# A length-six DFT over the sequence chunks for the third and fourth batch of a retention and Fourier-mixing kernel

## The chip, the core and the metric

The kernel runs on one core of a Trainium2 chip. The metric is the device time of one execution in microseconds (us): 241.95 us is the median of three runs before the change (241.94 to 242.2). The engines are called as in the profile: PE is TensorE (matmuls), PEld its weight loads, DVE is VectorE, ACT is ScalarE, POOL is GpSimd, SP is SyncE, which issues most DMAs.

## The reference

Four batches, eight heads, 768 positions, head width 64. A retention recurrence gives y; its heads, side by side, are a matrix x of 768 rows and 512 columns per batch. Then comes a two-dimensional Fourier transform whose real part is added, a normalisation over the columns and a two-layer MLP of width 2048.

```python
for t in range(S):
    state = gamma[None, :, None, None] * state + np.einsum('bhd,bhe->bhde', k[:, :, t], v[:, :, t])
    y[:, :, t] = scale * np.einsum('bhd,bhde->bhe', q[:, :, t], state)
...
X = np.fft.fft(x, axis=1)
X = np.fft.fft(X, axis=2)
mixed = np.real(X).astype(np.float32)
u = x + mixed
mu = np.mean(u, axis=-1, keepdims=True)
var = np.mean((u - mu) ** 2, axis=-1, keepdims=True)
un = (u - mu) / np.sqrt(var + 1e-06)
ch = np.maximum(un @ w_ch1, 0.0) @ w_ch2
return (u + ch).astype(np.float32)
```

## The kernel before

The 768 rows are six chunks of 128 rows. Batch 0's attention comes first, in an order written out by hand. After that, period b (b = 0 to 3) runs the MLP of batch b on PE and, in between, attention and Fourier mixing of batch b + 1.

**The order.** `emit` collects units of work in streams, each with a first and last due time in periods, spreads a stream's units evenly over that time, and emits all units by due time. The MLP of one period is 58 units of major work: 16 `h_unit` (four matmuls into psh, L1087), one `rstd_unit`, 12 `ch_unit` (four matmuls into psc, L1130), and the same again for the second half of the rows. A 58th of a period is called a turn here. The steps of attention for batch b + 1 share one stretch of due times (`TS1`, from 0.048 to 0.633 of a period) in proportion to their number of units. A scheduler then gives each engine its instructions in order of emission among those that it takes to be ready; it decides this when the program is built, and an engine runs its list strictly in that order. In the trace, PE's order follows the due times: y of pair 2, due at turn 25.4, stands right after the major unit that is due at turn 25.

Attention works on four pairs of heads. `cast_unit` (POOL) makes f16 copies, `t_unit` transposes them (for batches 2 and 3 by DMA from SP's queue), `a_unit` makes the masked products atm (PE wkA L664, DVE L667), `kv_unit` the states s (PE wkK L683, ACT L689, DVE L693), `y_unit` the result (PE wkY L714 and L718), which ACT writes into x (L726).

**The fold.** With n = 128 c + p the position (chunk c, row p) and k the frequency, `fold_s` (DVE, L743) makes x[c] + x[c + 3] for even k and x[c] - x[c + 3] for odd k, three chunks of each: the tile ab, on two sides of the columns. It runs in two parts, one after the third pair of heads (step 4) and one after the fourth (step 5). `fold_d` (DVE, L770) adds and subtracts the two sides into eo, `fold_e` (DVE, L784 and L786) folds once more into ee, which takes over ab's memory. `g0_unit` treats the column 0 apart: small sums xg (L879, L882), nine small matmuls (L891) and the result g0 (L897, L900).

**First stage.** `s1_unit` multiplies ee by the cosine table csp or the sine table ssp (L847): per quarter (e, cb), for even and odd k, three chunks of 193 columns are summed in PSUM. ACT copies the 386 columns into g, even and odd k interleaved (L854), DVE writes the mirrored copy gr (L858).

**Second stage.** `s2_unit` transforms over the columns (PE pq L1009, ACT L1011 and L1012, DVE u L1016 and L1019, POOL u L1037 and L1039) for one block of 128 rows, `norm_unit` takes mean and variance (DVE bst L1049, L1050) and centres the row (ACT un L1051), `unT_unit` transposes it into unT (for batches 2 and 3 by DMA, L1070). The first three blocks of batch b + 1 come at the end of period b, since `h_unit` of period b + 1 needs all three of them; the other three follow in the period itself. On POOL the casts of the next attention stand behind the u sums, and on SP the transposition of their q (qTz, L609) stands in the same queue as unT.

**Evictions.** psh has three buffers. In the second half of the rows ACT (L1091) takes ten of the sixteen psh and DVE (L1093) rows 1, 2, 4, 5, 8 and 13. psc goes out through DVE (ob, L1134) and SP.

Of the kernel before, what the change touches and what calls it, by code (L numbers as in the profile page):

```python
# [11 lines left out]
AF = mybir.ActivationFunctionType  # L12
ALU = mybir.AluOpType
f32 = mybir.dt.float32
f16 = mybir.dt.float16
# [4 lines left out]
P = 128  # L20
# [5 lines left out]
NHP = H // 2  # L26
NK = 193
KN = 2 * NK
XW = 260
MAGIC = 12582912.0  # L30
PAIR_ORDER = [0, 1, 3, 2]
# [16 lines left out]
ON_ACT = {'q': (0, 1, 0), 'kv': (1, 1, 1), 'g': (0, 1, 1), 'gr': (0, 0, 0)}  # L48
# [5 lines left out]
LD0, LD1 = (0.223, 0.312), (-0.370, 0.140)  # L54
HT0 = (0.666, 0.693, 0.632, 0.590)
NPE = 2
KD = (2, 3)
NT = 0.6
ACT_ROWS = ((2, 5, 6, 7, 8, 9, 10, 14), (0, 3, 6, 7, 9, 10, 11, 12, 14, 15), (2, 4, 5, 6, 7, 8, 10, 11, 13, 14))
# [3 lines left out]
def kernel(  # L63
# [9 lines left out]
    nc = tc.nc  # L73
# [15 lines left out]
    gp = pool("gp", 1)  # L89
# [6 lines left out]
    ps_g = pool("ps_g", 5, space=PSUM)  # L96
# [7 lines left out]
    csp = const.tile([P, 2, 3, NK], f16, tag="csp")  # L104
    ssp = const.tile([P, 2, 3, NK], f16, tag="ssp")
# [58 lines left out]
    ht16 = hp_.tile([P, NFB, 384], f16, tag="ht16")  # L164
# [565 lines left out]
    fd = {}  # L730

    def fold_s(b, lo, hi, s0, s1):
        def run():
            x = xts[b % 2]
            if b not in fd:
                fd[b] = dict(
                    ab=fp.tile([P, 2, 3, 2, XW], f16, tag="xab", name="xab"),
                    eo=fp.tile([P, 2, 2, 3, 256], f16, tag="eo", name="eo"),
                    g=gp.tile([P, 4, KN], f16, tag="g16", name="g16"),
                    gr=gp.tile([P, 4, 384], f16, tag="g16r", name="g16r"))  # L740
            ab = fd[b]["ab"]
            for a, op in ((0, ALU.add), (1, ALU.subtract)):
                nc.vector.tensor_tensor(out=ab[:, a, :, s0:s1, lo:hi],  # L743
                                        in0=x[:, 0:3, s0:s1, lo:hi],
                                        in1=x[:, 3:6, s0:s1, lo:hi], op=op)
        return run

    def fold_p(i):
        def run():
            h = 2 * ORD0[i]  # L750
            if 0 not in fd:
                fd[0] = dict(
                    ab=fp.tile([P, 2, 3, 2, XW], f16, tag="xab", name="xab"),
                    g=gp.tile([P, 4, KN], f16, tag="g16", name="g16"),
                    gr=gp.tile([P, 4, 384], f16, tag="g16r", name="g16r"))
            x, ab = xts[0], fd[0]["ab"]
            side = h // 4
            lo, hi = {0: (1, 129), 2: (129, 258), 4: (130, 258), 6: (2, 130)}[h]
            for a, op in ((0, ALU.add), (1, ALU.subtract)):
                nc.vector.tensor_tensor(out=ab[:, a, :, side, lo:hi],  # L760
                                        in0=x[:, 0:3, side, lo:hi],
                                        in1=x[:, 3:6, side, lo:hi], op=op)
        return run

    def fold_d(b, cb, es=(0, 1)):
        def run():
            ab, eo = fd[b]["ab"], fd[b]["eo"]
            i0 = 2 + 128 * cb
            for e in es:
                nc.vector.tensor_tensor(out=eo[:, e, :, :, 128 * cb:128 * cb + 128],  # L770
                                        in0=ab[:, :, :, 0, i0:i0 + 128],
                                        in1=ab[:, :, :, 1, i0:i0 + 128],
                                        op=(ALU.add, ALU.subtract)[e])
        return run

    def fold_e(b, e):
# [56 lines left out]
    def s1e_unit(e, cb, eng):  # L833
        def run():
            gi = 2 * e + cb
            dst = fd[0]["g"][:, gi].rearrange("p (i t) -> p t i", t=2)
            (nc.scalar.copy if eng == "a" else nc.vector.tensor_copy)(dst, fd[0]["s1", e, cb])
        return run

    def s1_unit(b, e, cb):  # L840
        def run():
            eo, g, gr = fd[b]["eo"], fd[b]["g"], fd[b]["gr"]
            tab = csp if e == 0 else ssp
            ps = ps_g.tile([P, 2, NK], f32, tag="g", name="ps1", padded_shape=[P, 2, 256])
            for par in range(2):
                for sb in range(3):
                    nc.tensor.matmul(ps[:, par, :],  # L847
                                     fd[b]["ee"][:, 2 * e + cb, par, sb, :] if b >= FB else
                                     eo[:, e, par, sb, 128 * cb:128 * cb + 128],
                                     tab[:, par, sb, :], start=(sb == 0), stop=(sb == 2))  # L850
            gi = 2 * e + cb
            dst = g[:, gi].rearrange("p (i t) -> p t i", t=2)
            if e == 0 or ON_ACT["g"][min(b, 2)]:
                nc.scalar.copy(dst, ps)  # L854
            else:
                nc.vector.tensor_copy(dst, ps)
            if b:
                (nc.scalar.copy if ON_ACT["gr"][min(b, 2)] else nc.vector.tensor_copy)(  # L858
                    gr[:, gi], g[:, gi, 384:0:-1])
        return run  # L860
# [4 lines left out]
    def g0_unit(b, parts=(0, 1, 2)):  # L865
        def run():
            for part in parts:
                (g0_a, g0_b, g0_c)[part](b)
        return run
# [34 lines left out]
    lb = {}  # L904
# [177 lines left out]
    def h_unit(b, rt, fb):  # L1082
        def run():
            unT = lb[b]["unT"]
            psh = ps_pm.tile([P, 384], f32, tag="pm", name="psh", padded_shape=[P, DM])
            for cb in range(4):
                nc.tensor.matmul(psh, w116[:, cb, fb * P:(fb + 1) * P],  # L1087
                                 unT[:, cb, rt * 384:(rt + 1) * 384],
                                 start=(cb == 0), stop=(cb == 3))
            if fb in ACT_ROWS[2 if (b, rt) == (B - 1, 0) else rt]:  # L1090
                nc.scalar.activation(ht16[:, fb, :], psh, AF.Relu, bias=0.0, scale=-1.0)  # L1091
            else:
                nc.vector.tensor_scalar(out=ht16[:, fb, :], in0=psh, scalar1=-1.0, scalar2=0.0,  # L1093
                                        op0=ALU.mult, op1=ALU.max)
        return run
# [61 lines left out]
    def attn_steps(b):  # L1157
        steps = []
        for step in range(6):
            un = []  # L1160
            if step < 4:
                un.append(held(cast_unit(b, step)))
            i = step - 1
            if 0 <= i < 4:
                un.append(kv_unit(b, i))
            i = step - 2
            if 0 <= i < 4:
                un.append(y_unit(b, i))
                if i == 2:
                    un += [fold_s(b, 0, 130, 0, 2), fold_d(b, 0)]  # L1170
                    if b < FB:
                        un += [g0_unit(b), s1_unit(b, 0, 0), s1_unit(b, 1, 0)]
            if step < 4:
                un.append(t_unit(b, step))
            i = step - 1
            if 0 <= i < 4:
                if b == 0:
                    un += [a0_unit(b, i, 0), a0_unit(b, i, 1)]
                else:
                    un += [a_unit(b, i, part) for part in range(3)]  # L1180
            if step == 5:
                un += [fold_s(b, 130, 258, 0, 2), fold_d(b, 1)]
                if b >= FB:
                    un += [g0_unit(b), fold_e(b, 0), fold_e(b, 1)]
            steps.append(un)
        return steps

# [88 lines left out]
    for b in range(B):  # L1276
# [15 lines left out]
        if b + 1 < B:  # L1292
            steps = attn_steps(b + 1)
            if b == 0:
                streams.append(([load_unit(1, i, 6) for i in range(4)], LD0[0], LD0[1]))
                streams.append(([qt_zeros], 0.1, 0.15))
                streams.append(([half_tables], HT0[0], HT0[1]))
                streams.append(([pad_unit], HT0[2], HT0[3]))
                ts = TS0
            else:  # L1300
                streams.append(([load_unit(b + 1, i) for i in range(4)], b + LD1[0], b + LD1[1]))
                n = [len(u) for u in steps[1:]]
                ts = list(TS1[:2]) + [TS1[2] + TS1[3] * sum(n[:j]) / sum(n) for j in range(6)]
            streams.append((steps[0], b + ts[0], b + ts[1]))
            streams += [(u, b + ts[j + 2], b + ts[j + 3]) for j, u in enumerate(steps[1:])]
            end = b + ts[-1]
            da = DA0 if b == 0 else DA1
            streams.append(([s1_unit(b + 1, e, cb) for cb in range(2) for e in range(2)
                             if cb or b + 1 >= FB], end + da[0], end + da[1]))
            streams += mix_units(b + 1, [0, 1, 2], *(end + t for t in da[2:]))  # L1310
# [31 lines left out]
```

## Time and profile before

| what | value |
|---|---|
| median of three runs | 241.95 us |
| profiled execution, its own time | 242.19 us |
| span of the instructions in it | 240.2 us |
| granted TensorE clock | 1.00 |
| first-stage matmuls of batches 1, 2, 3 (L847) | 72 matmuls, 8.1 us in all |
| DVE fold of batches 1, 2, 3 (L743, L770, L784, L786) | 36 operations, 18.9 us in all |

The span counts from the first to the last instruction; the profiled execution's own time is that of the run in which the profile was taken. "x24" is a count, "mean ns" the duration of one; what stands in brackets behind an instruction is the idle time of its engine just before it and what ended that. Matmuls are pipelined, so a row's duration of one matmul is longer than its pace; the pace is read from the chain, which gives a run of matmuls as one piece.

### The profile page before, as it was taken

The numbers are of one execution on the slowest core, as the hardware profiler recorded it, in microseconds if no ns is written. First come the engines' busy times: TensorE is split into PE (matmuls) and PEld (weight loads), VectorE is DVE, ScalarE is ACT, GpSimd is POOL, SyncE is SP. The second block draws the span as 40 slices with busy tenths as digits, with TensorE's granted clock in tenths as the row PEclk, the third lists the DMA queues.
The fourth block names the chain that finished last, engine by engine and source line by source line (L and its number), as shares of the span: only waits on it lengthen the run. The fifth ranks groups of instructions, "written<-read, shape, count | busy, mean of one in ns | idle before, by whom it ended". The sixth has DMA issues, their size and how long they took to land.

```text
span 240.2 us, 5238 instructions
## 1 busy us (share of the span) xinstructions
PE 228.5 (95%) x1999; PEld 142.6 (59%) x1999; DVE 172.8 (72%) x419; ACT 120.8 (50%) x268; POOL 81.6 (34%) x148
## 2 busy tenths in 40 slices
PE   0888999999999999999999999999999999999994
PEld 0366779756774646665557446655675455446543
DVE  8789987968898789977995749977886557315121
ACT  5989759674865544941248406722366227203400
POOL 8377802675300097850001808930003224000000
PEclk9999999999999999999999999999999999999999
DMA  7999999999999399979999587675100331221012
GB/s 179 232 271 266 209 206 207 209 246 247 233 231 216 65 202 217 192 142 136 257 275 208 106 182 207 130 117 153 44 3 0 84 115 23 44 90 44 1 44 87
DMA packets 100808, 36.77 MB, mean 153 GB/s; under 512 B 91440, under 2 KB 97840, under 8 KB 100784
## 3 DMA queue, kind: packets, MB, share of 16 engines
q1 hardware_dynamic: 96560, 32.25, 63.7%
q0 software_dynamic: 4224, 4.19, 10.5%
q8 instruction: 15, 0.25, 0.4%
q14 instruction: 9, 0.07, 0.1%
HBM read 27.26 MB, written 6.29 MB: 140 GB/s over the span
## 4 chain that ended last, share of the span: by engine, by line
PE 83%; DVE 5%; SPq 5%; DMA 3%; POOL 2%; ACT 1%; issue 1%; ACTq 0%; POOLq 0%; DVEq 0%
PE psc L1130 34%; PE psh L1087 28%; SPq L216 5%; PE psh L1104 3%; PE wkA L664 3%; DMA q<-in_q_dram 3%; PE ps L847 3%; PE wkY L718 2%; PE pq L1009 2%; PE wkY L714 1%; PE wkK L683 1%; PE ps L827 1%; PE tq L620 1%; PE pst L1074 1%; DVE u L931 1%
## 5 line engine op out<-in xcount | busy, mean ns | idle before, releaser
L1130 PE MATMUL psc<-w,ht 128*128 128x512 f16 (+2 forms) x400 | 88.9, 370 | 0.0
L1087 PE MATMUL psh<-unT,w 128*128 128x384 f16 x448 | 81.6, 326 | 0.3 <-ACT ht L1091 0.3
L1130 PEld LDWEIGHTS <-ht 128*128 128x128 f16 x400 | 37.6, 98 | 36.8
L1087 PEld LDWEIGHTS <-w 128*128 128x128 f16 x448 | 42.1, 98 | 24.2 <-issue 0.8
L1091 ACT ACTIVATE ht<-psh 128x384 f16<-128x384 f32 x66 | 31.7, 490 | 41.2 <-PE psh L1087 40.3
L1037 POOL TENSOR_TENSOR u<-u,x 128x256 f32<-128x256 f32 x21 | 13.4, 636 | 107.1 <-DVE u L1016 95.0
L1134 DVE SCALAR_TENSOR_TENSOR ob<-psc,stats,u 128x512 f32<-128x512 f32 (+2 forms) x25 | 18.1, 724 | 29.0 <-PE psc L1130 28.9
L1093 DVE TENSOR_SCALAR ht<-psh 128x384 f16<-128x384 f32 x46 | 25.3, 549 | 8.9 <-PE psh L1087 8.5
L667 DVE TENSOR_TENSOR atm<-wkA,maskp 128x512 f16<-128x512 f32 x36 | 23.6, 681 | 1.5 <-PE wkA L664 1.5
L1051 ACT ACTIVATE un<-u,stats 128x512 f16<-128x512 f32 x21 | 14.8, 719 | 12.2 <-DVE stats L1050 8.2
L1049 DVE BATCH_NORM_STATS2 bst<-u 128x6 f32<-128x512 f32 x21 | 14.4, 687 | 4.9 <-POOL u L1039 4.7
L693 DVE SCALAR_TENSOR_TENSOR s<-s,gk,wkK 128x128 f16<-128x128 f16 x48 | 16.2, 337 | 2.4 <-ACT s L689 1.6
L726 ACT ACTIVATE x<-wkY,gexp 128x384 f16<-128x384 f32 x24 | 12.9, 581 | 9.0 <-PE wkY L718 8.9
L438 POOL TENSOR_SCALAR kd<-k,gexp 128x384 f16<-128x384 f32 x24 | 13.9, 589 | 3.4 <-DMA k<-in_k_dram 3.1
L1039 POOL TENSOR_TENSOR u<-u,x 128x256 f32<-128x256 f32 x21 | 13.3, 636 | 0.0
L664 PE MATMUL wkA<-qTz,kT 128*128 128x256 f16 x72 | 13.2, 272 | 0.1
L1011 ACT COPY qn<-pq 128x128 f32<-128x128 f32 x18 | 4.9, 274 | 13.7 <-PE pq L1009 13.6
L1104 PEld LDWEIGHTS <-w 128*128 128x128 f16 x192 | 11.0, 98 | 0.9 <-issue 0.5
L1104 PE MATMUL psh<-unT,w 128*128 128x128 f16 x192 | 11.4, 219 | 0.1
L1016 DVE SCALAR_TENSOR_TENSOR u<-pq,g,qn 128x256 f32<-128x256 f32 x18 | 8.5, 473 | 3.2 <-PE psh L1087 2.5
L443 POOL TENSOR_SCALAR v<-v 128x768 f16<-128x768 f32 x12 | 10.0, 834 | 1.5 <-DMA v<-in_v_dram 1.5
L664 PEld LDWEIGHTS <-kT 128*128 128x128 f16 x72 | 6.9, 98 | 5.6 <-issue 0.5
(175 smaller groups left out, 310.4 us busy)
## 6 DMA issues: line engine op xcount, KB each, us to landing
q<-in_q_dram SPq DMA_DIRECT2D x16, 384.0 KB, 6.0
k<-in_k_dram SPq DMA_DIRECT2D x16, 384.0 KB, 5.6
v<-in_v_dram SPq DMA_DIRECT2D x16, 384.0 KB, 6.2
out_dram<-ob SPq DMA_DIRECT2D x23, 256.0 KB, 2.4
w<-in_moe_w_ch_dram POOLq DMA_DIRECT2D x8, 512.0 KB, 10.7
unT<-un SPq DMA_TRANSPOSE x15, 2.4
out_dram<-ob SPq DMA_DIRECT2D x1, 192.0 KB, 1.9
kT<-kd SPq DMA_TRANSPOSE x10, 3.1
```

What stands on the lines that cost most here:

```text
L438: kc = nc.gpsimd.tensor_scalar(out=kd[:, :, h2, :], in0=k32[:, h2], scalar1=gkd[:, h0 + h2:h0 + h2 + 1], scalar2=1.0, op0=ALU.mult, op1=AL ...
L664: mm = nc.tensor.matmul(wk[:, c2], st["kT"][:, c, :], st["qT"][:, :, c, :], start=True, stop=True)
L667: nc.vector.tensor_tensor(out=st["atm"][:, 2 * part:2 * part + 2], in0=wk, in1=maskp[:, PAIR_ORDER[i]].unsqueeze(1).to_broadcast([P, 2, 2, ...
L693: nc.vector.scalar_tensor_tensor(out=s16[:, c], in0=s16[:, c - 1], scalar=gk2[:, hp:hp + 1], in1=wk[:, c - c0], op0=ALU.mult, op1=ALU.add)
L1049: nc.vector.bn_stats(bst, u[:, kb, :])
L1051: nc.scalar.activation(un, u[:, kb, :], AF.Identity, bias=stats[:, kb, 0:1], scale=-1.0)
L1087: nc.tensor.matmul(psh, w116[:, cb, fb * P:(fb + 1) * P], unT[:, cb, rt * 384:(rt + 1) * 384], start=(cb == 0), stop=(cb == 3))
L1091: nc.scalar.activation(ht16[:, fb, :], psh, AF.Relu, bias=0.0, scale=-1.0)
L1093: nc.vector.tensor_scalar(out=ht16[:, fb, :], in0=psh, scalar1=-1.0, scalar2=0.0, op0=ALU.mult, op1=ALU.max)
L1104: mm = nc.tensor.matmul(psh[:, f], w116[:, cb, fb * P:(fb + 1) * P], unT[:, cb, kb * P:(kb + 1) * P], start=(cb == 0), stop=(cb == 3))
L1130: nc.tensor.matmul(psc[:, c0:c1], ht16[:, fb, rb3 * P:(rb3 + 1) * P], w216[:, fb, c0:c1], start=(fb == 0), stop=(fb == NFB - 1))
L1134: nc.vector.scalar_tensor_tensor(out=ob[:, c0:c1], in0=psc[:, c0:c1], scalar=lb[b]["st"][:, rb, 3:4], in1=lb[b]["u"][:, rb, c0:c1], op0=AL ...
```

## The change

For batches 2 and 3 (`SIX = 2`) the sum over the chunks becomes a DFT of length six: with k = 6 j + r, the residue r alone decides how the six chunks are added, and one matmul per real or imaginary part with a table of 128 rows remains. `fold_s` stays and makes the first butterfly; the new `fold_six` makes the rest of it, in place in ab, one half of 128 columns at a time, between `fold_s` and `fold_d`. It has six DVE operations and one ACT copy per half. The first step of `g0_unit` (xg) moves ahead of the second `fold_six`, which overwrites what it reads. `s1_unit` multiplies by new tables: the first run of 65 columns belongs to r = 0 or 3, the other two runs of 130 to r = 2 and 4 or to r = 1 and 5. PSUM holds six runs of 65 columns, and ACT writes them into g at a step of six. The tables lie over the memory of csp and ssp for chunks 1 and 2, which nothing reads after batch 1; four units make them in period 1, due from 1.30 to 1.5, each with one POOL memset and four small ACT operations that stand behind the last ACT eviction of the first sixteen psh. All due times stay, but the three units that each of the two batches gains share the same stretch of `TS1`.

```diff
+KG = 390
+SIX = 2
+SIXP = 0
+ST0 = (1.30, 1.5)
...
-                    g=gp.tile([P, 4, KN], f16, tag="g16", name="g16"),
+                    g=gp.tile([P, 4, KG], f16, tag="g16", name="g16"),
...
+    def six_of(par):
+        return [t[:, par, 1:3].rearrange("p c k -> p (c k)") for t in (csp, ssp)]
+
+    def six_table(e, par):
+        def run():
...
+            to = six_of(par)[e]
...
+            nc.gpsimd.memset(to[:, 64:325], 0.0)
+            for out, in_, m in ((to[:, 0:65 - par], one, 1.0),
+                                (pairs[0], src[:, r0:r1 + 1:r1 - r0], 0.5),
+                                (pairs[1][:, 0], alt[:, r0], sg),
+                                (pairs[1][:, 1], alt[:, r1], -sg)):
+                if SIX > 1:
+                    with tc.issue_after(lb[SIX - 1]["relu"].ins):
+                        nc.scalar.activation(out, in_, AF.Copy, bias=0.0, scale=m)
...
+    def fold_six(b, half):
+        def run():
+            ab, eo = fd[b]["ab"], fd[b]["eo"]
+            c0 = 2 + 128 * half
+            a = [ab[:, :, c, :, c0:c0 + 128] for c in range(3)]
+            t = ab[:, :, 0, :, 2:130] if half else eo[:, 0, :, 0:2, 128:256]
+            nc.vector.tensor_tensor(out=t, in0=a[1], in1=a[2], op=ALU.add)
+            nc.vector.tensor_tensor(out=a[2], in0=a[1], in1=a[2], op=ALU.subtract)
+            for par, z, op, inv in ((0, t, ALU.subtract, ALU.add),
+                                    (1, a[2], ALU.add, ALU.subtract)):
+                (nc.gpsimd if SIXP else nc.vector).scalar_tensor_tensor(
+                    out=a[1][:, par], in0=a[0][:, par], scalar=2.0,
+                                               in1=z[:, par], op0=ALU.mult, op1=op)
+                nc.vector.tensor_tensor(out=a[0][:, par], in0=a[0][:, par], in1=z[:, par], op=inv)
+            nc.scalar.copy(a[2][:, 1], t[:, 1])
+        return run
...
+            if b >= SIX:
+                ps = ps_g.tile([P, 6, 65], f32, tag="g", name="ps1", padded_shape=[P, 6, 80])
+                for par in range(2):
+                    z, to = fd[b]["ee"][:, 2 * e + cb, par], six_of(par)[e]
+                    two = ps[:, 1:6:4] if par else ps[:, 2:5:2]
+                    for sb, (o, w, out) in enumerate(((0, 65, ps[:, 3 * par]), (65, 130, two),
+                                                      (195, 130, two))):
+                        nc.tensor.matmul(out, z[:, sb, :], to[:, o:o + w],
+                                         start=par == sb == 0, stop=par == 1 and sb == 2,
+                                         skip_group_check=True)
+                gi = 2 * e + cb
+                (nc.scalar.copy if e == 0 or ON_ACT["g"][min(b, 2)] else nc.vector.tensor_copy)(
+                    g[:, gi].rearrange("p (j r) -> p r j", r=6), ps)
...
-                    un += [fold_s(b, 0, 130, 0, 2), fold_d(b, 0)]
+                    un += [fold_s(b, 0, 130, 0, 2)]
+                    if b >= SIX:
+                        un.append(fold_six(b, 0))
+                    un.append(fold_d(b, 0))
...
-                un += [fold_s(b, 130, 258, 0, 2), fold_d(b, 1)]
+                un.append(fold_s(b, 130, 258, 0, 2))
+                if b >= SIX:
+                    un += [g0_unit(b, (0,)), fold_six(b, 1)]
+                un.append(fold_d(b, 1))
                 if b >= FB:
-                    un += [g0_unit(b), fold_e(b, 0), fold_e(b, 1)]
+                    un += [g0_unit(b, (1, 2) if b >= SIX else (0, 1, 2)), fold_e(b, 0),
+                           fold_e(b, 1)]
...
+                streams.append(([six_table(e, par) for e in range(2) for par in range(2)], *ST0))
```

More of the change, by code (lines that the diff above doesn't have):

```diff
@@ L753, in run @@
                     ab=fp.tile([P, 2, 3, 2, XW], f16, tag="xab", name="xab"),
-                    g=gp.tile([P, 4, KN], f16, tag="g16", name="g16"),
+                    g=gp.tile([P, 4, KG], f16, tag="g16", name="g16"),
                     gr=gp.tile([P, 4, 384], f16, tag="g16r", name="g16r"))
@@ L773, in run @@
                                         op=(ALU.add, ALU.subtract)[e])
+        return run
[3 more added lines that the diff above has]
+        def run():
+            same, other = (csp, ssp) if e == 0 else (ssp, csp)
+            sg = (-1.0 if e == 0 else 1.0) * math.sqrt(0.75)
+            to = six_of(par)[e]
+            src, alt = (t[:, par, 0, 0:192].rearrange("p (j r) -> p r j", r=3)
+                        for t in (same, other))
+            r0, r1 = ((1, 2), (0, 2))[par]
+            pairs = [to[:, o:o + 130].rearrange("p (r j) -> p r j", r=2)[:, :, 0:64]
+                     for o in (65, 195)]
+            one = same[:, 0, 0, 0:193:3] if par == 0 else src[:, 1]
+            nc.gpsimd.memset(to[:, 64:325], 0.0)
[6 more added lines that the diff above has]
+                        nc.scalar.activation(out, in_, AF.Copy, bias=0.0, scale=m)
+                else:
+                    nc.gpsimd.tensor_scalar(out=out, in0=in_, scalar1=m, scalar2=1.0,
+                                            op0=ALU.mult, op1=ALU.mult)
+        return run
@@ L835, in run @@
             gi = 2 * e + cb
-            dst = fd[0]["g"][:, gi].rearrange("p (i t) -> p t i", t=2)
+            dst = fd[0]["g"][:, gi, 0:KN].rearrange("p (i t) -> p t i", t=2)
             (nc.scalar.copy if eng == "a" else nc.vector.tensor_copy)(dst, fd[0]["s1", e, cb])
@@ L843, in run @@
             tab = csp if e == 0 else ssp
+            if b >= SIX:
[11 more added lines that the diff above has]
+                    g[:, gi].rearrange("p (j r) -> p r j", r=6), ps)
+                (nc.scalar.copy if ON_ACT["gr"][min(b, 2)] else nc.vector.tensor_copy)(
+                    gr[:, gi], g[:, gi, 384:0:-1])
+                return
             ps = ps_g.tile([P, 2, NK], f32, tag="g", name="ps1", padded_shape=[P, 2, 256])
@@ L851, in run @@
             gi = 2 * e + cb
-            dst = g[:, gi].rearrange("p (i t) -> p t i", t=2)
+            dst = g[:, gi, 0:KN].rearrange("p (i t) -> p t i", t=2)
             if e == 0 or ON_ACT["g"][min(b, 2)]:
@@ L1090, in run @@
             if fb in ACT_ROWS[2 if (b, rt) == (B - 1, 0) else rt]:
-                nc.scalar.activation(ht16[:, fb, :], psh, AF.Relu, bias=0.0, scale=-1.0)
+                relu = nc.scalar.activation(ht16[:, fb, :], psh, AF.Relu, bias=0.0, scale=-1.0)
+                if rt == 0:
+                    lb[b]["relu"] = relu
             else:
```

## The prediction

> **What bounds the kernel now.** I read the page's busy shares, the granted clock and the chain that ended last.
>
> ```profile
> span 240.2 us, 5238 instructions
> PE 228.5 (95%) x1999; PEld 142.6 (59%) x1999; DVE 172.8 (72%) x419; ACT 120.8 (50%) x268; POOL 81.6 (34%) x148
> PEclk9999999999999999999999999999999999999999
> PE 83%; DVE 5%; SPq 5%; DMA 3%; POOL 2%; ACT 1%; issue 1%; ACTq 0%; POOLq 0%; DVEq 0%
> ```
>
> TensorE bounds the span as a whole, at full clock. The change touches two stretches of it: the fold of batch 2, beside the major work of batch 1, and the fold of batch 3, beside that of batch 2. So next come the busy times by stretch (PE, PEld, DVE, ACT, POOL).
>
> ```profile
> 104.30:112.40 8.10, 8.10 (x68) 4.63 (x67) 5.29 (x12) 1.59 (x4) 1.00 (x2) 1.00 1.10 167
> 112.40:126.40 14.00, 13.94 (x127) 8.43 (x126) 12.84 (x31) 4.75 (x10) 0.00 (x0) 1.00 1.12 240
> 126.40:142.40 16.00, 16.00 (x102) 8.88 (x99) 8.38 (x22) 7.65 (x19) 6.54 (x11) 1.00 0.82 156
> 164.40:178.10 13.70, 13.70 (x127) 8.46 (x126) 12.69 (x31) 4.71 (x10) 0.00 (x0) 1.00 0.17 62
> ```
>
> While batch 2 is folded, PE has no gap, but VectorE is busy 12.84 of 14.00 us (batch 3: 12.69 of 13.70): nearly full too, and this is where the change adds VectorE work. Is anything of PE's waiting on the end of that fold? The first weight loads of the next batch's MLP answer it.
>
> ```profile
> 142.43 1.09 PEld L1087 LDWEIGHTS <-w 128*128 128x128 f16 x8 [0.39 <-DMA unT<-un]
> 193.89 1.29 PEld L1087 LDWEIGHTS <-w 128*128 128x128 f16 x8
> ```
>
> At 142.43 the loader of batch 2 stood 0.39 us for the transposed rows unT, with PE still fed by the matmul in the array. The chain behind unT, read back from there:
>
> ```profile
> 138.34 2.83 SPq L1070 DMA_TRANSPOSE unT<-un  x2
> 136.82 1.43 SPq L609 DMA_TRANSPOSE qTz<-q16z  x1
> 135.80 0.99 POOL L435 TENSOR_SCALAR q16z<-q 128x384 f16<-128x384 f32 x2
> 135.19 0.64 POOL L1039 TENSOR_TENSOR u<-u,x 128x256 f32<-128x256 f32 x1
> 133.41 0.64 POOL L1037 TENSOR_TENSOR u<-u,x 128x256 f32<-128x256 f32 x1 [1.19 <-DVE u L1016]
> 132.26 0.69 DVE L1049 BATCH_NORM_STATS2 bst<-u 128x6 f32<-128x512 f32 x1 [0.49 <-POOL u L1039]
> 130.43 0.48 DVE L1016 SCALAR_TENSOR_TENSOR u<-pq,g,qn 128x256 f32<-128x256 f32 x1 [1.27 <-PE psh L1087]
> 129.37 0.39 PE L1009 MATMUL pq<-gk,g 128*128 128x129 f16 x4
> 126.73 2.13 ACT L854 CAST g<-ps 128x386 f16<-128x386 f32 x4
> 125.87 0.56 DVE L786 TENSOR_TENSOR ee<-eo 128x768 f16<-128x768 f16 x1
> ```
>
> The last fold result ee is done at 126.43, the first second-stage product starts at 129.37, the u of the third block leaves POOL at 135.83, its casts hold the SP queue's qTz until 136.82, and both unT stand behind qTz. So for batch 2 the unT chain and PE arrive together: slack 0. For batch 3 the last unT is issued at 191.11:
>
> ```profile
> 191.11 1.22 SPq L1070 DMA_TRANSPOSE unT<-un  x1
> DMA to landing us min/median/max: 2.4/2.4/2.5
> ```
>
> It lands at 193.5, and the loader at 193.89 waited for nothing: slack about 0.35 us. My reading is that each period ends at the later of two things: PE's own work and the landing of unT.
>
> **The change part by part.** *First-stage matmuls.* 24 per batch stay 24; 193 columns become 65 (8 of them) or 130 (16).
>
> ```profile
> 126.18 2.05 PE ps L847 x24
> 113.31 0.35 PE wkY L718 x12
> 38.62 7.27 PE psh L1104 x128
> 112.15 0.86 PE psc L1130 x4
> L847 PEld LDWEIGHTS <-ee 128*128 128x128 f16 x72 | 6.1, 98 | 0.7 <-DVE ee L784 0.5
> L847 PE MATMUL ps<-csp,ee 128*128 128x193 f16 x36 | 4.1, 248 | 0.0
> ```
>
> Each of these loads weights of its own. 64 columns come at 0.35/12 = 29 ns, 128 at 7.27/128 = 57 ns. A quarter (six matmuls) is then 2 x 29.6 + 4 x 57.7 = 0.29 us, 1.16 per batch against 2.05: PE saves 0.89 a batch, 1.78 in all. [...]
>
> *VectorE.* Per half of 128 frequencies fold_six adds two adds of 512 elements, two of 256, two scalar_tensor_tensor of 256, and one ACT copy of 256 that the next fold_d waits for. Nothing is removed.
>
> ```profile
> L770 DVE TENSOR_TENSOR eo<-xab 128x768 f16<-128x768 f16 x12 | 6.1, 552 | 0.1
> L760 DVE TENSOR_TENSOR xab<-x 128x384 f16<-128x384 f16 x6 | 1.9, 357 | 0.3 <-ACT x L596 0.2
> 115.68 1.03 DVE L770 TENSOR_TENSOR eo<-xab 128x768 f16<-128x768 f16 x2
> L1016 DVE SCALAR_TENSOR_TENSOR u<-pq,g,qn 128x256 f32<-128x256 f32 x18 | 8.5, 473 | 3.2 <-PE psh L1087 2.5 <-ACT qn L1012 0.6
> L693 DVE SCALAR_TENSOR_TENSOR s<-s,gk,wkK 128x128 f16<-128x128 f16 x48 | 16.2, 337 | 2.4 <-ACT s L689 1.6
> L802 ACT ACTIVATE ht<-x 128x128 f16<-128x128 f16 x2 | 0.6, 304 | 0.0
> L508 ACT COPY kT<-tq 128x768 f16<-128x768 f16 x4 | 3.2, 802 | 0.0
> ```
>
> The adds cost (552 - 357)/384 = 0.51 ns an element: 422 ns at 512, 292 at 256. No all-f16 scalar_tensor_tensor is in the trace. Its bounds are 292 (as the add) and 473 (L1016); L693, partly f16, lies on the line of the f32 ones, so I take 473. Sum 2 x 422 + 2 x 292 + 2 x 473 = 2.37 us, less 0.074 of overlap each (two adds take 1.03, not 1.10) = 1.93 per half, 3.9 per batch. The copy is 304 + 128 x 0.78 = 0.40, with the two hand-overs about 0.5; in the first half atm products fill it, in the second nothing sure does. Total 4.4 us a batch.
>
> *What hides it.* The three extra units per batch squeeze the same stretch of due times: kv to fold of step 4 come due 1.5 to 1.9 turns earlier (y of pair 2 at 23.5 instead of 25.4 turns, fold_e unchanged at 36.7). At 0.86 us a turn the first half starts 1.6 us sooner, into VectorE time that is free (104.3 to 112.4: 5.29 of 8.10 busy). Another 0.7 is idle later:
>
> ```profile
> 120.69 0.56 DVE L1093 TENSOR_SCALAR ht<-psh 128x384 f16<-128x384 f32 x1 [0.69 <-PE psh L1087]
> ```
>
> So ee is late by 4.4 - 1.6 - 0.7 = 2.1 us. Between ee and pq lie 2.9 us now, with eight psh matmuls (1.3 us) in them. If those run before the late s1, pq follows ee after a quarter (0.29 + 0.25), a g copy (0.60) and a load: 1.2 us, and is late by 0.4; if PE's order stays, by 2.1 - 0.9 = 1.2. I take 0.8. From pq on the chain (POOL's six u sums, casts, qTz, unT) keeps its length, so unT is 0.8 late. Batch 2 has no slack: +0.8. Batch 3 has 0.35: +0.45. The saving of 1.78 is not collected, since PE would only stand longer for unT; it does pay for eviction waits of up to 1.7 us in the h phase, where fold_six stands before the L1093 evictions on VectorE and PE can run three psh ahead.
>
> *At nothing.* Sixteen table operations on ACT (up to 130 elements, so at most L802's 0.3 us, some 4 us together) and four memsets on POOL (261 elements, half of L243's 0.5 us) come due between turns 75 and 87, at least eight us ahead of use:
>
> ```profile
> 112.12 0.27 ACT L689 CAST s<-wkK 128x128 f16<-128x128 f32 x1 [4.30 <-issue]
> 118.46 0.49 ACT L1091 ACTIVATE ht<-psh 128x384 f16<-128x384 f32 x1 [3.88 <-PE psh L1087]
> L243 POOL MEMSET ht<- 128x512 f16 x1 | 0.5, 515 | 0.0
> 130.99 0.64 POOL L1037 TENSOR_TENSOR u<-u,x 128x256 f32<-128x256 f32 x1 [25.70 <-DVE u L1016]
> ```
>
> ACT idles 4.3 and 3.9 us there, POOL 25.7. Without that cover, all in front of one s copy, batch 2 would pay up to 4. The g copies take 390 elements for 386 with a wider output step: 0 to 0.1 us each, inside the 0.4 margin. The xg sums move ahead of fold_six: same count, no queue behind them but PE's nine small matmuls, now earlier.
>
> **Sum.** 242.19 (profiled execution, span 240.2) + 0.8 + 0.45 = 243.4; the median of the runs is 0.24 lower: 243.2.
>
> **The rivals.** *Faster, the saving arrives.* If the freed VectorE time takes both halves and the u sums close up (POOL stands 1.19 us before the second block at 133.41, because bst at 132.26 holds the next u behind it on VectorE), unT comes 0.9 earlier in both batches and PE collects 1.78: 240.2. It decides once pq is under 0.3 late and the gap closes. For it: that gap, and 2.8 free us before 112.4. Against: fold_six's second half has no earlier slot.
>
> *The scalar_tensor_tensor runs as fast as an add.* 292 instead of 473 ns, four a batch: 0.7 less, ee 1.4 late, unT 0.1: 242.19 + 0.1 - 0.25 - 0.24 = 241.8, no change. Against it L693's place on the slow line. [...]
>
> *VectorE becomes the bound.* If the earlier turns give nothing (wkA of pair 3 or y held by its own data), ee is 3.7 late, pq at least 2.0 in either order; +2.0 and +1.65: 245.6. It decides once ee comes over about 3 us late, since then all psh are done and PE has only psc and then unT. With no overlap of the operations and both copies exposed ee is 5.0 late: +3.3 and +2.95, 248.2. For it: 12.84 of 14.00 busy.
>
> *The matmuls don't get shorter.* If loads at 98 ns pace them, the last quarter is 0.3 longer: +0.3 a batch, 243.8. Against: 29 ns at 64 columns.
>
> **How the numbers follow.** Forecast 0.40 (own range 242.5 to 244.5), VectorE bound 0.20, saving arrives 0.24 (240.2 to 241.4), fast scalar_tensor_tensor or other cancelling 0.13, no shorter matmuls 0.03. 0.2% is 0.48 us, about what this kernel's runs can tell. Faster 0.26, the same 0.14, slower 0.60. The range 240.4 to 246.6 leaves out the far ends of both.
>
> **What would show it.** Right: matmuls L847's successors at 29 and 58 ns pace; fold_six 1.9 us a half; ee about 2 us later against PE's turns; at the first h weights of batches 2 and 3 a loader wait for unT of over 1 us, now with PE idle. Wrong: no such wait (the saving then shows as PE's shorter path), PE idle in the h phase before an L1093 eviction (then VectorE bounds there), or ACT's table operations in front of an s copy.

## The result and the profile after

| | before | changed kernel |
|---|---|---|
| median of six runs | 241.99 us (241.82 to 242.2) | 253.17 us (251.11 to 255.26) |
| ratio | 1 | 1.0452, 95% interval 1.042 to 1.0483 |
| profiled execution, its own time | 242.19 us | 253.34 us |
| its span | 240.2 us | 251.2 us |

The change costs 11.2 us where 1.2 were forecast. The page of the changed kernel shows a dent in PE's clock that was not there before, and less of the ending chain on PE:

```profile
span 251.2 us, 5286 instructions
PE 231.5 (92%) x1999; PEld 141.8 (56%) x1999; DVE 180.6 (72%) x443; ACT 131.3 (52%) x288; POOL 82.7 (33%) x152
PEclk9999999999999999999997999999997999999999
PE 68%; DVE 13%; ACT 7%; DMA 5%; POOL 3%; issue 2%; SPq 1%; ACTq 0%; POOLq 0%; DVEq 0%
```

The two slices at 7 lie at about 135 and 192 us, where the first stage of batches 2 and 3 hands over to the second. The windows there (PE, PEld, DVE, ACT, POOL, granted clock):

```profile
128.30:137.50 9.20, 5.92 (x44) 3.44 (x43) 4.52 (x13) 7.42 (x11) 1.86 (x4) 0.81 0.83 150
185.50:194.10 8.60, 5.30 (x44) 3.19 (x43) 4.40 (x13) 7.38 (x11) 1.44 (x3) 0.88 0.00 0
```

PE stands 3.28 and 3.30 us there and then runs under a reduced clock, while ACT, which was busy 7.65 of 16.00 us in the corresponding stretch before, is the engine at work. What ACT does, in its timeline (start, duration; in brackets the idle time before):

```profile
128.30 1.48 ACT L903 CAST g<-ps 128x390 f16<-128x390 f32 x1 [0.30 <-PE ps L899]
129.40 0.70 ACT L1155 ACTIVATE ht<-psh 128x384 f16<-128x384 f32 x1
130.00 4.05 ACT L903 CAST g<-ps 128x390 f16<-128x390 f32 x3
134.43 0.27 ACT L1075 COPY qn<-pq 128x128 f32<-128x128 f32 x1 [0.38 <-PE pq L1073]
```

and who waits for it, on PE:

```profile
129.84 0.23 PE L1073 MATMUL pq<-gk,g 128*128 128x129 f16 x1
129.91 0.49 PE L1151 MATMUL psh<-unT,w 128*128 128x384 f16 x2
132.80 0.29 PE L1073 MATMUL pq<-gk,g 128*128 128x128 f16 x2 [2.40 <-ACT g L903]
132.93 0.32 PE L1151 MATMUL psh<-unT,w 128*128 128x384 f16 x1
134.10 0.29 PE L1073 MATMUL pq<-gk,g 128*128 128x128 f16 x1 [0.85 <-ACT g L903]
```

The groups by shape give the reason. The changed kernel's copy into g, beside the copy of the old form that batch 1 still makes (L918):

```profile
L903 ACT CAST g<-ps 128x390 f16<-128x390 f32 x8 | 11.1, 1581 | 0.6 <-PE ps L899 0.6
L918 ACT CAST g<-ps 128x386 f16<-128x386 f32 x4 | 2.2, 600 | 3.3 <-PE ps L911 3.3
```

390 elements at a step of six take 1.58 us, 386 at a step of two 0.60. All four quarters of a batch pass through this one engine, so by the durations the last g is some 4 x 0.98 = 3.9 us late. In the timeline, where the copies overlap and one eviction stands between them, the four take 5.75 us from 128.30 to 134.05, for 2.13 before: 3.6 us. The other pieces came as costed or a little below:

```profile
L813 DVE TENSOR_TENSOR xab<-xab 128x512 f16<-128x512 f16 x2 | 0.8, 419 | 0.0
L817 DVE SCALAR_TENSOR_TENSOR xab<-xab 128x256 f16<-128x256 f16 x6 | 2.3, 418 | 0.0
L820 DVE TENSOR_TENSOR xab<-xab 128x256 f16<-128x256 f16 x6 | 1.5, 284 | 0.0
L821 ACT COPY xab<-eo 128x256 f16<-128x256 f16 x2 | 0.8, 405 | 7.5 <-DVE xab L820 7.5
L801 ACT ACTIVATE ssp<-csp 128x64 f16<-128x64 f16 x4 | 0.9, 261 | 0.0
```

One thing is left: the clock. One-us windows show it:

```profile
131.00:132.00 1.00, 0.00 (x0) 0.00 (x0) 0.26 (x1) 1.00 (x2) 0.00 (x0) 1.00 1.35 221
135.00:136.00 1.00, 1.00 (x8) 0.69 (x6) 0.78 (x2) 0.55 (x3) 0.53 (x1) 0.50 0.07 16
138.00:139.00 1.00, 1.00 (x6) 0.48 (x5) 0.95 (x4) 0.31 (x2) 0.49 (x2) 1.00 0.00 0
```

PE stands from 130.4 on but for 0.45 us of matmuls, and from 134.0 the granted clock is 0.50 for 3.41 us; the same from 192.0, after the second batch's copies. The 3.41 us ahead of the two falls:

```profile
130.57:133.98 3.41, 0.45 (x3) 0.17 (x3) 0.99 (x3) 3.41 (x3) 0.00 (x0) 1.00 1.11 200
188.59:192.00 3.41, 1.10 (x9) 0.64 (x10) 1.25 (x4) 3.09 (x5) 0.00 (x0) 1.00 0.00 0
```

In such a stretch four psh matmuls take 1.28 us of the chain (at 135.78), for 0.65 at full clock (at 60.63): half speed, and for 3.41 us of it 1.7 us of PE lost. So in this execution each batch pays about 3.3 for standing and 1.7 for the clock, 10.0 us for both. Another 0.67 is one wait of PE, in its timeline at the start of batch 2's fold:

```profile
116.01 0.38 PE L668 MATMUL wkA<-qTz,kT 128*128 128x256 f16 x2 [0.67 <-DMA qTz<-q16z]
```

That is 10.7 us, and the span is 10.9 longer than in run 1 below, whose copies alone differ (251.2 against 240.3). Beside the kernel before, where the spans are 11.0 apart, the count does not close: the shorter matmuls should have saved 1.78, and what takes that back is not in it.

### The profile page after: what moved, and what is told of

Read it like the earlier page. It is cut to its first block, busy times and chain, and to the rows that moved or that the text cites. A ratio compares the mean times of both kernels' runs of the same rounds, so it can differ in the third digit from the quotient of the medians.

```text
span 251.2 us, 5286 instructions
## 1 busy us (share of the span) xinstructions
PE 231.5 (92%) x1999; PEld 141.8 (56%) x1999; DVE 180.6 (72%) x443; ACT 131.3 (52%) x288; POOL 82.7 (33%) x152
## 4 chain that ended last, share of the span: by engine, by line
PE 68%; DVE 13%; ACT 7%; DMA 5%; POOL 3%; issue 2%; SPq 1%; ACTq 0%; POOLq 0%; DVEq 0%
PE psc L1196 28%; PE psh L1151 22%; ACT g L903 4%; PE psh L1170 3%; DMA v<-in_v_dram 3%; PE wkA L668 3%; DMA qTz<-q16z 3%; PE pq L1073 2%; PE wkY L722 2%; DVE xab L747 1%; DVE atm L671 1%; PE wkY L718 1%; SPq L220 1%; PE wkK L687 1%; PE ps L875 1%
## 5 line engine op out<-in xcount | busy, mean ns | idle before, releaser
L1196 PE MATMUL psc<-w,ht 128*128 128x512 f16 (+2 forms) x400 | 89.8, 373 | 0.0
L1151 PE MATMUL psh<-unT,w 128*128 128x384 f16 x448 | 84.4, 331 | 0.3 <-ACT ht L1155 0.3
L1159 DVE TENSOR_SCALAR ht<-psh 128x384 f16<-128x384 f32 x46 | 25.3, 550 | 8.4 <-PE psh L1151 8.0
L903 ACT CAST g<-ps 128x390 f16<-128x390 f32 x8 | 11.1, 1581 | 0.6 <-PE ps L899 0.6
L1073 PE MATMUL pq<-gk,g 128*128 128x128 f16 (+2 forms) x36 | 5.0, 261 | 6.6 <-ACT g L903 6.5
## 6 DMA issues: line engine op xcount, KB each, us to landing
w<-in_moe_w_ch_dram POOLq DMA_DIRECT2D x8, 512.0 KB, 10.7
out_dram<-ob SPq DMA_DIRECT2D x1, 192.0 KB, 1.9
```

Source lines behind the costliest of these rows:

```text
L903: (nc.scalar.copy if e == 0 or ON_ACT["g"][min(b, 2)] else nc.vector.tensor_copy)(g[:, gi].rearrange("p (j r) -> p r j", r=6), ps)
L1151: nc.tensor.matmul(psh, w116[:, cb, fb * P:(fb + 1) * P], unT[:, cb, rt * 384:(rt + 1) * 384], start=(cb == 0), stop=(cb == 3))
L1196: nc.tensor.matmul(psc[:, c0:c1], ht16[:, fb, rb3 * P:(rb3 + 1) * P], w216[:, fb, c0:c1], start=(fb == 0), stop=(fb == NFB - 1))
```

## The experiments

The theory after the result: the write of g at a step of six is dear, and almost all of the 11.2 us hangs on it. The rivals: fold_six on VectorE (the prediction's own mechanism), the tables, the clock by itself. Each run is compared with runs of the kernel before on the same chip, whose medians were about 242.2 us. Edits are against the changed kernel unless said otherwise.

**1. The copy turned round.** g is written at step one, and the step lies on the PSUM side.

```diff
-                    g[:, gi].rearrange("p (j r) -> p r j", r=6), ps)
+                    g[:, gi].rearrange("p (j r) -> p j r", r=6), ps.rearrange("p r j -> p j r"))
```

> The changed kernel, in which only the order of elements in ACT's copy of the first stage into g is turned round for batches 2 and 3: it writes g at a step of one element and reads PSUM at a step of one run, where it wrote at a step of six elements. Same elements, same 390, and the same order of instructions on all engines. Theory (the output step sets the copy's 1.58 us, and PE's wait for four such copies with the half clock that follows sets the loss): the copy falls to 0.7 us or less, no half clock in the fold stretches, time 241 to 244. Rival 1 (the late ee, from fold_six on VectorE, sets the loss and the copies only fill the same wait): the copy gets cheaper, but the time stays over 248. Rival 2 (PSUM's layout of six padded runs or their shortness sets the copy's price): the copy stays over 1.2 us and the time over 250.

Measured: 242.64 us (242.32 to 243.1), ratio 1.0017, 95% 1.0008 to 1.0026. The copy's group and the two windows in this kernel:

```profile
L903 ACT CAST g<-ps 128x390 f16<-128x390 f32 x8 | 3.5, 490 | 0.7 <-PE ps L899 0.6
128.30:137.50 9.20, 9.20 (x67) 5.00 (x67) 7.22 (x20) 5.94 (x16) 6.16 (x11) 1.00 0.78 146
185.50:194.10 8.60, 8.60 (x41) 3.92 (x40) 3.84 (x10) 2.25 (x4) 1.60 (x3) 1.00 0.40 108
```

The instructions and their order on every engine are those of the changed kernel; only the direction of eight copies differs. 1.58 us became 0.49, PE has no gap there, the clock stays at 1.00, and 253.17 - 242.64 = 10.5 us are gone. The copy's write is the cause, and the half clock came only with it.

**2. The dear write in the kernel before.** For batches 2 and 3 the old fold stays, but ACT writes 384 columns of g at a step of six, which puts them in another order.

```diff
-            dst = g[:, gi].rearrange("p (i t) -> p t i", t=2)
+            dst, ps = (g[:, gi].rearrange("p (i t) -> p t i", t=2), ps) if b < 2 else (g[:, gi, 0:384].rearrange("p (j t q) -> p t q j", t=2, q=3), ps[:, :, 0:192].rearrange("p t (q j) -> p t q j", q=3)); b < 2 or nc.gpsimd.memset(g[:, gi, 384:386], 0.0)
```

> The kernel before, in which for batches 2 and 3 ACT's copy into g writes 384 of the 386 columns at a step of six elements in six runs of 64 (the columns then stand in another order, so the result differs; POOL clears the last two). Nothing else of the change is in it. Theory: the copy takes 1.4 to 1.6 us instead of 0.60, pq comes some 3.5 us later, PE stands 2 to 3 us in each of the two batches and then runs at half clock for a few us; time 248 to 252. Rival 1 (fold_six sets the loss): under 244. Rival 2 (not the step, but the layout of the changed kernel's PSUM tile): copy under 0.8 us, time within 0.5 of before.

Measured: 248.56 us (247.18 to 251.08), ratio 1.0243, 95% 1.0213 to 1.0273. Groups and PE's waits in the profiled execution, which took 251.08 us:

```profile
L854 ACT CAST g<-ps 128x384 f16<-128x384 f32 x8 | 10.6, 1610 | 0.0
PE pq L1009 <- ACT g L854: 4.4, 4, 1.2
```

The step is dear without anything else of the change. Two of the four runs kept a mean granted clock of 1.000 and took 247.18 and 247.75 us, so without any half clock the cost is 5.0 to 5.5 us. The other two took 249.36 us at 0.993 and, in the profiled execution with two stretches of half clock of 3.41 us, 251.08 at 0.986. So the clock by itself, the last rival, is the smaller part.

**3. No fold_six, dear copy.** Both calls are left out, so the six chunks are not combined fully.

```diff
-                    if b >= SIX:
-                        un.append(fold_six(b, 0))
...
-                    un += [g0_unit(b, (0,)), fold_six(b, 1)]
+                    un += [g0_unit(b, (0,))]
```

> The changed kernel without fold_six (the other butterflies are left out, so the result differs); the new tables, shorter matmuls and the copy at a step of six stay. Theory (copies set the loss): copies still 1.5 us, ee some 2.5 us earlier, PE still waits for the copies, time 248 to 252. Rival 1 (fold_six sets the loss): 240 to 243.

Measured: 250.32 us (248.54 to 253.1), ratio 1.031, 95% 1.0283 to 1.0338; the copies still take 1.64 us each and PE still waits 6.0 us for them. Of the 11.2 us only some 2.9 go with fold_six, less than the spread of either kernel's runs, and most of the 2.9 is the clock: at the same mean clock of 0.993 the changed kernel took 251.11 us and this one 250.31 and 250.32, 0.8 apart. fold_six does not set the loss.

**4. No fold_six, copy turned round.** Edits 1 and 3 together.

> The changed kernel with the copy turned round as in the first of these runs and without fold_six (result differs): what is left are tables, shorter matmuls and the shifted due times. Theory: 240 to 241.5, the saving of PE as far as unT lets it through; the difference to the first run is the whole price of fold_six, 1 to 3 us. Rival (earlier due times or table operations cost something by themselves): over 242.

Measured: 241.83 us (241.5 to 243.55), ratio 0.9991, 95% 0.9978 to 1.0005. Beside run 1, fold_six costs 242.64 - 241.83 = 0.8 us for both batches. The tables, which are still made here, cost nothing that the time shows. Yet even without fold_six, little of the 1.78 us that PE saves arrives. The chain shows the saving, the loader's timeline one of the places where it ends:

```profile
126.25 1.20 PE ps L899 x24
141.63 1.09 PEld L1151 LDWEIGHTS <-w 128*128 128x128 f16 x8 [0.37 <-DMA unT<-un]
```

24 matmuls take 1.20 us, as costed (1.16). At the next batch's first weights PE is 0.80 us ahead of the kernel before, and its loader already waits for unT.

**5. fold_six's last copy on DVE.** With edit 1.

```diff
-            nc.scalar.copy(a[2][:, 1], t[:, 1])
+            nc.vector.tensor_copy(a[2][:, 1], t[:, 1])
```

> The first run's kernel (copy into g turned round), with the last copy of fold_six made by VectorE in place of ACT (4 copies of 256 f16 elements). Theory that the hand-over from VectorE to ACT and back delays the fold and keeps ACT from psh (ACT stood 7.5 us in all in front of these copies): ee 0.3 to 0.5 us earlier, 242.0 to 242.4. Rival (the hand-over is covered by atm and evictions, and VectorE only gets more to do): 242.5 to 242.9, as the first run.

Measured: 243.18 us (242.81 to 243.98), ratio 1.0037, 95% 1.0021 to 1.0053. The DVE copy takes 0.22 us for ACT's 0.41, and still nothing is gained, so the hand-over shows no cost of its own. The time is even 0.3 above the rival's range. A PE wait of 0.65 us for qTz, which run 1's profile does not have, is in this one; whether it makes the difference is not shown.

**6. Half of the dear copies on DVE.** Here the copies write at step six as in the changed kernel.

```diff
-                (nc.scalar.copy if e == 0 or ON_ACT["g"][min(b, 2)] else nc.vector.tensor_copy)(
+                (nc.scalar.copy if cb == 0 else nc.vector.tensor_copy)(
```

> The changed kernel as it is (copies still write g at a step of six), but two of the four copies of each batch, those with cb = 1, run on DVE. Theory A (the step-six write is dear on ACT alone, through its own write path): DVE's copies take 0.4 to 0.7 us, ACT's keep 1.6; the eight split 4 and 4, pq comes about 2 us earlier per batch than in the changed kernel, and the time is 245 to 247.5 us. Rival B (the price lies in the strided 16-bit write as such, whichever engine writes): DVE's copies take 1.2 us or more each, the two engines share the delay, and since DVE is nearly full there the time is 247 to 250 us. What decides is the duration of the DVE copies.

Measured: 248.05 us (247.61 to 248.79), ratio 1.0241, 95% 1.0222 to 1.026. The line's two groups (minimum, median and maximum in ns):

```profile
L903 ACT CAST g<-ps x4: 1454/1470/1487, 127.7 to 184.5; 128x390 f16<-128x390 f32 x4
L903 DVE CAST g<-ps x4: 1450/1451/1453, 129.4 to 186.3; 128x390 f16<-128x390 f32 x4
```

DVE pays 1.45 us for the same write, where its step-one evictions of 384 elements (L1159) take 0.55: the price is not ACT's alone. The mechanism and the time are B's. With two engines at the copies PE stands only 1.97 us in the ten from 128 on, and its clock stays at 1.00 there in the profiled execution:

```profile
128.00:138.00 10.00, 8.03 (x62) 4.30 (x61) 8.66 (x20) 5.82 (x12) 3.92 (x7) 1.00 0.63 118
```

**7. The due times as before.** Edit 1, and the three extra units of each batch are joined to their neighbours, so that nothing is squeezed.

```diff
-                        un.append(fold_six(b, 0))
+                        un.append(lambda u=un.pop(), w=fold_six(b, 0): (u(), w()))
...
-                    un += [g0_unit(b, (0,)), fold_six(b, 1)]
+                    un.append(lambda u=un.pop(), w=g0_unit(b, (0,)), z=fold_six(b, 1): (u(), w(), z()))
```

> The first run's kernel, with fold_six joined to fold_s (and to the first step of g0) in one unit, so that the attention steps of batches 2 and 3 keep the due times of the kernel before. Theory A (the squeezed due times cost PE 0.3 to 0.6 us a batch, because y now stands ahead of its last atm): PE's waits for atm go, 241.7 to 242.3. Theory B (the squeeze is what hides the first half of fold_six, as the prediction has it): ee comes over 1 us later than in the first run, unT with it, 243.3 to 245.

Measured: 245.03 us (244.79 to 245.96), ratio 1.0118, 95% 1.0093 to 1.0144. The loader, and the last ee of batch 2, first here and then in run 1:

```profile
144.03 1.09 PEld L1151 LDWEIGHTS <-w 128*128 128x128 f16 x8 [1.10 <-DMA unT<-un]
129.95 0.56 DVE L834 TENSOR_TENSOR ee<-eo 128x768 f16<-128x768 f16 x1
```

```profile
128.14 0.55 DVE L834 TENSOR_TENSOR ee<-eo 128x768 f16<-128x768 f16 x1
```

ee is 1.8 us later than with the squeeze, and the mechanism that the prediction described appears: unT is late and the next batch's weights wait 1.10 us for it. The earlier due times are worth 245.03 - 242.64 = 2.4 us.

**8. The kernel before with its copies turned round**, for batches 1 to 3.

```diff
-            dst = g[:, gi].rearrange("p (i t) -> p t i", t=2)
+            dst, ps = g[:, gi].rearrange("p (i t) -> p i t", t=2), ps.rearrange("p t i -> p i t")
```

> The kernel before, with ACT's copy of the first stage turned round in the same way for batches 1 to 3 (output at a step of one element in place of two). Theory (an output step of two already costs 0.1 us a copy, and the copies lie in front of unT, which has no slack for batch 2): copies 0.49 instead of 0.60, time 0.1 to 0.6 lower. Rival (PE's own work sets the end): copies cheaper, time the same within 0.1.

Measured: 242.13 us (241.78 to 242.78), ratio 0.9996, 95% 0.9983 to 1.001. The copies fall from 0.60 to 0.48 us, and nothing follows from it: a step of two was cheap enough to be hidden.

```profile
L854 ACT CAST g<-ps 128x386 f16<-128x386 f32 x12 | 5.8, 481 | 3.7 <-PE ps L847 3.4
```

**9. Steps of four and eight** in the kernel before, as in run 2 (`w` is 2 for batch 2, 4 for batch 3; one run).

```diff
-            dst = g[:, gi].rearrange("p (i t) -> p t i", t=2)
+            w = {2: 2, 3: 4}.get(b); dst, ps = (g[:, gi].rearrange("p (i t) -> p t i", t=2), ps) if b < 2 else (g[:, gi, 0:384].rearrange("p (j t q) -> p t q j", t=2, q=w), ps[:, :, 0:192].rearrange("p t (q j) -> p t q j", q=w)); b < 2 or nc.gpsimd.memset(g[:, gi, 384:386], 0.0)
```

> The kernel before, whose copy into g writes 384 columns at a step of four elements for batch 2 and of eight for batch 3 (the columns stand in another order, so the result differs). If the price grows with the step: 1.0 to 1.2 us at four, over 1.9 at eight. If there is a threshold between two and six: 0.6 at four and 1.6 at eight, or 1.6 at both. Time 245 to 256 by what the copies cost.

Measured: 249.66 us. The line's groups:

```profile
L854 ACT CAST g<-ps x4: 1019/1130/1138, 127.1 to 129.6; 128x384 f16<-128x384 f32 x4
L854 ACT CAST g<-ps x4: 1875/2198/2211, 179.9 to 184.7; 128x384 f16<-128x384 f32 x4
```

For 384 to 390 f16 elements the copy takes 0.49, 0.60, 1.13, 1.6 and 2.2 us at steps of 1, 2, 4, 6 and 8: beyond two it grows by about 0.27 us per element of step.

**10. The last batch alone.** Edit 1, and batch 2 keeps the old fold.

```diff
-SIX = 2
+SIX = 3
...
-ST0 = (1.30, 1.5)
+ST0 = (2.30, 2.5)
```

> The changed kernel with the g copies turned round (written at step one, PSUM read at step six) and the length-six DFT for the last batch alone; batch 2 keeps the old fold, and the tables are made in period 2 instead of period 1. Theory A (the periods' gains and losses add up as in the ledger of the run with both batches turned round: period 1 ends 0.4 us ahead, period 2 gives back 0.5): without the first batch's gain the time is 242.3 to 242.8 us, no better than before. Rival B (batch 3 has slack at its unT and could collect the shorter first stage once it doesn't start from a shifted schedule): 241.3 to 241.8 us, faster than both kernels. The eight copies become four of about 0.49 us at step one and four of 0.60 us at step two.

Measured: 242.87 us (242.43 to 243.77), ratio 1.0022, 95% 1.0011 to 1.0032. Rival B falls; batch 3's own slack does not let the saving through. A's figure holds but for 0.1 us.

**11. The shared due times begun earlier**, with edit 1.

```diff
-TS1 = (-0.040, -0.020, 0.048, 0.585)
+TS1 = (-0.040, -0.020, 0.025, 0.608)
```

> The changed kernel with the g copies turned round and the attention's shared stretch of due times begun 0.023 of a period (1.3 turns) earlier, with the same end, so that the three extra units of each batch no longer squeeze y against its atm. Theory A (of the 1.78 us that the shorter first stage saves, the squeeze costs about 0.9 and fold_six 0.8): the small waits of y for atm go, fold_six stays as early as with the squeeze, and the time is 241.4 to 242.1 us. Rival B (the earlier units wait for their own inputs, the casts of POOL and the transposed q and k of the DMA queue): PE waits there instead, 242.6 to 243.5 us.

Measured: 243.58 us (243.43 to 244.62), ratio 1.0057, 95% 1.0044 to 1.007. Worse, as rival B has it; PE's waits in the profile (us in all, times, longest; its execution took 244.62 us, the slowest of the six) name the inputs of both theories:

```profile
PE wkY L722 <- DVE atm L671: 0.7, 3, 0.3
PE wkA L668 <- DMA qTz<-q16z: 0.6, 1, 0.6
```

**12. Two evictions of the fold's stretch from DVE to ACT**, with edit 1.

```diff
-ACT_ROWS = ((2, 5, 6, 7, 8, 9, 10, 14), (0, 3, 6, 7, 9, 10, 11, 12, 14, 15), (2, 4, 5, 6, 7, 8, 10, 11, 13, 14))
+ACT_ROWS = ((2, 5, 6, 7, 8, 9, 10, 14), (0, 3, 4, 6, 7, 8, 9, 10, 11, 12, 14, 15), (2, 4, 5, 6, 7, 8, 10, 11, 13, 14))
```

> The changed kernel with the g copies turned round and rows 4 and 8 of the second sixteen psh evicted by ACT instead of DVE (0.50 us on ACT instead of 0.55 on DVE each), which takes 1.1 us off DVE between the two halves of fold_six. Theory A (VectorE's fullness in that stretch makes ee late and is what fold_six costs): ee comes 0.5 to 1.1 us earlier per batch, the psh behind them don't wait, and the time is 241.5 to 242.3 us. Rival B (ee was not what PE waited for once the copies are cheap, and ACT's evictions come later than DVE's did): no change or slower, 242.5 to 243.5 us.

Measured: 242.89 us (242.69 to 243.22), ratio 1.0028, 95% 1.0017 to 1.0039. The last ee of batch 2 comes 0.37 us before run 1's, not 0.5 to 1.1, and the time does not follow:

```profile
127.77 0.56 DVE L834 TENSOR_TENSOR ee<-eo 128x768 f16<-128x768 f16 x1
```

So no version that computes the whole reference beat the kernel before by a measurable amount.

## Why the prediction was wrong

The direction came true, the size did not: 253.17 against 243.2 and a range up to 246.6. By the prediction's steps:

- *"The g copies take 390 elements for 386 with a wider output step: 0 to 0.1 us each, inside the 0.4 margin."* **This step failed.** Each copy grew from 0.60 to 1.58 us, by 1.0, and its cover was gone at once, since the four copies of a batch follow one another on ACT with PE's pq behind the last. The runs put 10.5 us on it (run 1). The trace of before held a hint: the prediction's rows have L1091 at 0.49 us for 384 elements at step one, and the old copy at step two takes 0.60 (L918 above). Those 0.11 us per element of step, carried on to six, give 0.49 + 5 x 0.11 = 1.04: still too little, but far outside the margin. The bound of 0.1 had no row behind it.
- *The half clock* was no step of the prediction: after the start no row of before showed PE standing for long, and a stall was priced at its own length. In the profiled execution it came to half as much again.
- *Matmuls* at 29 and 58 ns: right, 24 in 1.20 us (run 4) for a predicted 1.16.
- *fold_six* at 1.93 us a half: right. The chain gives the first half of batch 3 in the changed kernel as 0.34 + 0.44 + 0.76 + 0.40 = 1.94:

```profile
172.15 0.34 DVE eo L813
172.52 0.44 DVE xab L814
172.98 0.76 DVE xab L817 x2
173.74 0.40 DVE xab L820 x2
```

  scalar_tensor_tensor lies at 418 ns, between the 292 and 473 taken as bounds and nearer to the one chosen; the rival in which it runs as fast as an add falls.
- *The squeeze hides the first half, and ee comes 2.1 us late*: right. With the copy mended ee ends at 128.69 against 126.43, 2.3 us late; without the squeeze (run 7) 4.1, where the time is 245.03. That is the rival "VectorE becomes the bound", which had 3.7 and 245.6 for this condition.
- *unT 0.8 and 0.45 us late, and PE waiting for it*: wrong but for run 7, where the weights waited 1.10 us. In the changed kernel PE itself was later than unT. In run 1, with the copy mended, the last unT of batch 2 were issued 0.85 us earlier than in the kernel before (137.49 for 138.34), and that of batch 3 0.45 earlier (190.66 for 191.11), although ee was 2.3 us late. That the chain from pq on "keeps its length" did not hold: POOL's 1.19 us of standing in front of the second block's u sums is gone, so the six run without a gap:

```profile
132.53 0.64 POOL L1101 TENSOR_TENSOR u<-u,x 128x256 f32<-128x256 f32 x1
137.49 2.85 SPq L1134 DMA_TRANSPOSE unT<-un  x2
```

  This is the condition of the rival "the saving arrives", and still PE did not collect.
- *The saving is not collected*: right in the outcome, but not for the reason given, since in run 1 nothing waits for unT. Even without fold_six only 0.2 to 0.4 us arrived, and that interval holds 1 (run 4).
- *Tables and memsets at nothing*: right, 0.25 to 0.33 us an operation on ACT. One copy of s (at 104.56) stands among them, which was named as a sign of being wrong, but no wait of PE for it is in the trace.

With the one step mended, the sum's 243.2 stands beside 242.64 measured in run 1. That is in part luck: the two terms that the sum adds, unT's 0.8 and 0.45, did not come. Where exactly run 1 spends the first stage's 1.78 us is settled only in part. Together with the 0.4 us by which run 1 is slower than the kernel before, some 2.2 us have to be found: 0.8 is fold_six, and 0.5 are waits of PE, which stands 0.55 us between 92 and 194 us, about half of it for atm in the squeezed stretch, where the kernel before stands 0.06. The rest stays open; the two attempts to win it back (runs 11 and 12) failed.

## What to carry to other kernels

A change of layout that only touches the address pattern of an eviction can have a price of its own (here 1.58 us a copy at step six for 0.60 at step two): find a row for that step, or bound it by the widest step the trace shows and carry the slope on; "a few elements more" is no bound. If a regrouping is needed, put the step on the PSUM side, where it cost nothing here (0.49 us a copy). And when several such copies stand in a row ahead of PE's next work, add to PE's stall the half clock that may follow it (here 1.7 us behind a stall of 3.3).

## What the runs showed of the hardware

- An f16 write into SBUF at a step cost both ACT and DVE time: 1.47 and 1.45 us for 390 elements at step six (run 6), and 0.49, 0.60, 1.13, 1.5 to 1.6 and 2.2 us on ACT at steps 1, 2, 4, 6 and 8. Reading PSUM at a step of 80 f32 with a write at step one took 0.49 us, as long as the contiguous 384-element evictions of psh.
- In the profiled execution of the changed kernel the clock fell to 0.50 for 3.41 us from 134.0 and again from 192.0, after 3.41 us that held 0.45 and 1.10 us of matmuls; its mean clock is 0.984, and those of runs 2 and 3 have 0.986 and 0.980. In run 6, where no 3.41 us around the copies held less than 1.46, it did not fall there. So PE did not stand for the whole time ahead of a fall; where the limit lies is not shown.
- The mean clock differs between runs of one kernel, and the time with it: the changed kernel took 251.11 us at 0.993 and 255.26 at 0.971, and two of the four runs of run 2 kept 1.000. What decides it is not shown.
